# Letting 128-row products run as four column tiles of 32, so that tiling runs join

## The chip, the cores and the metric

The kernel runs on one core of a Trainium2 chip. The metric is device time in microseconds (us), from the first to the last instruction of the program on that core. A core has a matrix engine (PE, TensorE), which multiplies a stationary operand that it has loaded (PEld) by a moving operand and writes to PSUM; a vector engine (DVE), a scalar engine (ACT), a general engine (POOL), and a queue (SP) that issues transfers by DMA.

PE can work as one array of 128 rows by 128 columns, or as several smaller arrays side by side: two row tiles of 64 rows, two column tiles of 64 columns, or four column tiles of 32 columns. Its tiling mode is a property of each product, and going from one mode to another costs something.

## The reference

Two layers of a recurrent, memory-augmented attention block (A) alternate with two gated feed-forward blocks (B), on 2048 tokens of 448 features; each block has a layer norm before it and a residual sum after it.

```python
# A: 64 segments of 32 tokens, one after another; 8 memory rows are carried along
for s in range(n_seg):
    h = concatenate([mem, xs])                   # 8 + 32 rows of 448
    q, k, v = h @ Wq, h @ Wk, h @ Wv             # 16 heads of 256
    p = softmax(where(mask, q @ k.T / 16, -1e9))
    o = (p @ v) @ Wo
    mem = o[:8]                                  # goes into the next segment
    outs.append(o[8:])
# B
gate, up = x @ W_gate, x @ W_up                  # 448 -> 1792
out = (gate * (gate > 0) * up) @ W_down          # 1792 -> 448
```

The loop over segments is serial through `mem`: a segment's memory rows need the whole attention of the segment before.

## The kernel before, in words

**Folded weights.** At the start the kernel multiplies Wq by Wk, and Wv by Wo, per head (`products` in `setup`), so that a step works with 448-wide matrices M and N alone. The weights are loaded in quarters, by transposing transfers (`wT`) and plain ones (`wo`), in the order in which the calls stand.

**Steps.** Both attention layers run in one loop of 68 steps, the second layer four segments behind the first. A step t does, in the code's names:

- `t_units`: h times M, as batches `tH` (two row tiles of 64, for the last 64 of the 448 features) and `tF` (full array, the other 384);
- `s_mem`, batch `smem`: scores of the memory rows, 5 products per layer of 40 columns (8 memory and 32 segment keys); softmax; `p_t_mem`, batch `ptm`: one transpose by a product with the identity;
- `u_mem` (`umem`, row tiles) and `un_mem` (`unm`): the value sums of the memory rows, 28 groups of four products, each on one column tile of 32 (mode COLS4);
- `m_t`, batch `mt`: five small transposing products that bring the new memory rows into the layout of the next step;
- `s_seg`, batch `sseg`: scores of the segment rows, 14 products per layer, most of 40 columns; softmax; `u_seg` (`useg`, row tiles);
- every second step `un` (`una`, `unb`): the value sums of two segments, groups of four column-tile products of 448 columns, and `glu` with batches `glH` (row tiles), `glF` (gate and up products, full array, 128 columns) and `dn` (down products, full array, 448 columns).

**Who sets the order.** Nothing is ordered by hand at run time: a planner (`_Order`) writes the order of every engine when the kernel is built. `turns` fixes the order of PE's batches by ranks (`RANK`) and by which batches are ready and have a PSUM bank. `run` then goes through time with estimated costs, adds `SWITCH` (100 ns) where a PE batch has another mode than the one before, and fills the other engines' orders. A batch is given to `mm` with a mode: FULL, ROWS, COLS2 or COLS4. One batch alone has an alternative: `mt` may run as ROWS where it comes after ROWS (the argument `alt`). Every matmul is issued in `_Sched.pe`, so all of them carry line 135 in the profile, and groups are told apart by their tiles: `hT,TTm` is smem, `hT,TTs` sseg, `ident,Pm` ptm, `selm,X` mt, `Nw,UTm` unm, `Nw,big` un, `xBT,big` glF (128 rows) or glH (64 rows), `big,hB` dn, `PTs,hK` useg, `PTm,hK` umem.

A batch waits for its semaphores at its first weight load and signals at its last matmul.

Of the kernel before, what the change touches and what calls it, by code (L numbers as in the profile page):

```python
# [13 lines left out]
D = 448  # L14
# [158 lines left out]
class _Order:  # L173
# [76 lines left out]
    def turns(self):  # L250
# [38 lines left out]
            fire(o)  # L289
        return order[::-1]  # L290

    def run(self):
        self.graph()
        free = {e: 0.0 for e in self.ENGS}
        mode = 0
        cand = {e: [] for e in self.ENGS}
        banks = {b: 0.0 for b in range(8)}
        bankt = {}

        def activate(o):  # L300
            o.ready = {e: self.ready_at(o, e) for e in o.eng}
            for e in o.eng:
                cand[e].append(o)

        for o in self.ops:
            if o.np == 0:
                activate(o)
        order = []
        turn = self.turns()
        total = len(self.ops)  # L310
        busy = {e: 0.0 for e in self.ENGS}
        last = self.LAST

        def at(o, e):
            t = o.ready[e]
            if t < free[e]:
                t = free[e]
            if o.alloc:
                n = len(o.alloc)
                if len(banks) < n:  # L320
                    return None
                x = sorted(banks.values())[n - 1] + last[e]
                if x > t:
                    t = x
            elif e != "pe":
                for tl, q in o.bq:
                    d = bankt.get((tl.bank, q))
                    if d:
                        for src, x in d.items():
                            if src != e and x + last[e] > t:  # L330
                                t = x + last[e]
            return t

        while len(order) < total:
            best = None
            for e in self.ENGS:
                lst = []
                for o in cand[e] if e != "pe" else turn[-1:]:
                    t = at(o, e) if o.np == 0 else None
                    if t is not None:  # L340
                        lst.append((t, o))
                if not lst:
                    continue
                lim = max(free[e], min(lst, key=lambda x: x[0])[0]) + SLACK[e]
                bt, bo = 0.0, None
                for t, o in lst:
                    if t <= lim and (bo is None or o.prio > bo.prio or (o.prio == bo.prio and o.i < bo.i)):
                        bt, bo = t, o
                if best is None or bt < best[0]:
                    best = (bt, e, bo)  # L350
            if best is None:
                raise RuntimeError("no operation can go: the buffers are held in a cycle")
            t, e, o = best
            if len(o.eng) > 1:
                for e2 in o.eng:
                    if e2 != e:
                        t2 = at(o, e2)
                        if t2 is not None and t2 + o.cost[e2][0] < t + o.cost[e][0]:
                            t, e = t2, e2
            for tl in o.alloc:  # L360
                b = min(banks, key=lambda k: (banks[k], k))
                del banks[b]
                tl.bank = b
                for q in ALLQ:
                    bankt[(b, q)] = {}
            dur, occ = o.cost[e]
            if e == "pe":
                turn.pop()
                if mode == o.alt:
                    o.mode = mode  # L370
                elif o.mode != mode:
                    dur += self.SWITCH
                    occ += self.SWITCH
                    mode = o.mode
            o.fixed = e
            o.start = t
            busy[e] += occ
            free[e] = t + occ
            o.fin = t + dur
            for tl, q in o.bq:  # L380
                d = bankt[(tl.bank, q)]
                if d.get(e, 0.0) < o.fin:
                    d[e] = o.fin
            for tl in o.tiles:
                tl.left -= 1
                if tl.left == 0:
                    banks[tl.bank] = max(max(bankt[(tl.bank, q)].values(), default=0.0) for q in ALLQ)
            for e2 in o.eng:
                cand[e2].remove(o)
            for q in o.succs:  # L390
                q.np -= 1
                if q.np == 0:
                    activate(q)
            order.append(o)
        self.span = max(o.fin for o in order)
        self.busy = busy
        self.order = order
# [155 lines left out]

def TR(out, src, ident):
    return (out, src, ident, dict(is_transpose=True))

# [3 lines left out]
class _Kernel:  # L562
# [222 lines left out]
    def setup(self):  # L785
# [72 lines left out]
        for q in range(4):  # L858
            products(q, (0, 1, 4, 5)[q], (2, 3, 6, 7)[q], True)
        wT(0, S.Wv_d, 0)  # L860
        wo(2, 0)
        wo(3, 1)
        wT(1, S.Wv_d, 1)
        wT(4, S.Wv_d, 2)
        wo(6, 2)
        wo(7, 3)
        wT(5, S.Wv_d, 3, half=0)
        wT(5, S.Wv_d, 3, half=1)
# [131 lines left out]
    def s_mem(self, t):  # L1000
# [3 lines left out]
        nl = l1 - l0  # L1004
        T = S.tile()

        def mms():
            out = []
            for l in range(l0, l1):
                v = T.b()[:, l * KEYS:l * KEYS + KEYS]  # L1010
                for c in range(3):
                    out.append(MM(v, S.TTm[:, l, c * 8:c * 8 + 8, :, :].rearrange("p i s q -> p (i s q)"), S.hT[:, b, c, l, 0:KEYS], start=(c == 0)))
                for odd in range(2):
                    w = S.TTm3[:, l, 1 - odd:17 - odd, :].rearrange("p i q -> p (i q)")
                    out.append(MM(v, w, S.hT[:, b, 3 + odd, l, 0:KEYS], stop=(odd == 1)))
            return out

        S.mm("smem", mms, nl * 5 * 25.0, [("TTm", k, st) for k in range(5) for st in range(2)] + S.hkeys(b), T.res())
        src = lambda: T.b()[:, l0 * KEYS:l1 * KEYS].rearrange("p (l x) -> p l x", l=nl)
        st, F = S.stat, S.Fm  # L1020
        dst = S.Pm[:, :].rearrange("p (l x) -> p l x", l=2)[:, l0:l1, 0:KEYS]
# [8 lines left out]
    def s_seg(self, t):  # L1030
# [3 lines left out]
        nl = l1 - l0  # L1034
        T = S.tile()

        def mms():
            v = T.b()[:, 0:8 * KEYS].rearrange("p (s g l x) -> p s g l x", s=2, g=2, l=2)
            out = []
            for l in range(l0, l1):  # L1040
                for g in range(2):
                    for c in range(3):
                        for st in range(2):
                            i = c * 8 + 4 * g
                            out.append(MM(v[:, st, g, l, :], S.TTs[:, l, st, i:i + 4, :].rearrange("p u q -> p (u q)"), S.hT[:, b, c, l, 0:KEYS], start=not out))
                    out.append(MM(v[:, :, g, l, :], S.TTs[:, l, g, 24:28, :].rearrange("p u q -> p (u q)"), S.hT[:, b, 3:5, l, 0:KEYS],
                                  stop=(l == l1 - 1 and g == 1)))
            return out

        S.mm("sseg", mms, nl * (12 * 25.0 + 2 * S.pitch(80)) + 12.0, [("TTs", k, st) for k in range(5) for st in range(2)] + S.hkeys(b), T.res())  # L1050
        full = nl == 2
        v = lambda ap: ap if full else ap[:, l0:8:2, :]
        src = lambda: v(T.b()[:, 0:8 * KEYS].rearrange("p (a x) -> p a x", a=8))
# [27 lines left out]
    def p_t_mem(self, t):  # L1081
        S = self
        T = S.tile()
        S.mm("ptm", lambda: [TR(T.b().bitcast(BF)[:, 0:128], S.Pm[:, :], S.ident[:, :])], 60.0, [("Pm",), ("ident",)], T.res())
        S.cp("ptmE", lambda: S.PTm[:, :], lambda: T.b().bitcast(BF)[:, 0:128], 128, T.res(), [("PTm",)], speed=1.9)

    def u_mem(self, t):
# [63 lines left out]
    def m_t(self, t):  # L1151
# [6 lines left out]
        T = S.tile()  # L1158
        def mms(mode):
            r = slice(0, 64 if mode == ROWS else 128)  # L1160
            return [MM(T.b()[:, 32 * i:32 * i + 32], S.X[r, c:c + 128], S.selm[r, :], start=True, stop=True) for i, c in enumerate((0, 128, 256, 384, 320))]

        S.mm("mt", mms, 5 * 25.0, [("X", 0), ("X", 1)] + [("sel", j) for j in range(3)], T.res(), alt=ROWS)
        for half, nb in ((0, 4), (1, 5)):
            r = slice(64 * half, 64 * half + 64)
            S.cp("mtE", lambda r=r, nb=nb: S.hT[r, b, 0:nb, l0:l1, SEG:KEYS],
# [83 lines left out]
    def glu(self, q, n):  # L1250
        S = self
        for k, (a, z) in enumerate(S.GU):
# [11 lines left out]

            S.mm(f"glH{k}", hm, w * S.pitch(n) + 8.0, [("xBT",), ("W3", 0), ("W3", 1)], G.res() + V.res() + [("hB", k)], mode=ROWS)
            for W, T, nm in ((S.Wg, G, "Wg"), (S.Wu, V, "Wu")):
                S.mm(f"glF{k}", lambda W=W, T=T, a=a, w=w, col=col: [MM(col(T, i), W[:, kt, (a + i) * 128:(a + i) * 128 + 128], S.xBT[:, kt, 0:n], stop=(kt == 2))
                                                                 for i in range(w) for kt in range(3)],
                     3 * w * S.pitch(n), [("xBT",)] + [(nm, kt) for kt in range(3)], T.res())
            S.act("glE", lambda E, G=G, k=k, w=w: E.activation(S.gT[:, k % 2, 0:w * n], G.b()[:, 0:w * n], ACT.Relu), w * n, G.res(), [("gT", k % 2)])  # L1270
            S.dve("glE", lambda E, V=V, k=k, w=w, a=a: E.tensor_tensor(S.hB[:, a:a + w, 0:n], S.gT[:, k % 2, 0:w * n].rearrange("p (i x) -> p i x", i=w),  # L1271
                                                                        V.b()[:, 0:w * n].rearrange("p (i x) -> p i x", i=w), ALU.mult),
# [2 lines left out]
        wd = [("Wd", 0), ("Wd", 1)]  # L1275
        if n == 128:
            for k in range(7):
                S.mm("dn", lambda k=k: [MM(T.b()[:, 0:D], S.hB[:, f, :], S.Wd[:, f, :], start=(f == 0), stop=(f == NFC - 1)) for f in (2 * k, 2 * k + 1)],
                     2 * S.pitch(D), [("hB", k // 2)] + wd, T.res())
        else:  # L1280
            for k in range(7):
                S.mm("dnc", lambda k=k: [MM(T.b()[32 * j:32 * j + 32, 0:D], S.hB[:, 2 * k + j // 2, 32 * (j % 2):32 * (j % 2) + 32], S.Wd[:, 2 * k + j // 2, :],
# [102 lines left out]
```

## Time and profile before

Three runs: median 1495.27 us (1492.01 to 1495.7). The profiled execution has a span of 1494.6 us.

| engine | busy us | share | instructions |
|---|---|---|---|
| PE, matmuls | 1451.1 | 97% | 37105 |
| PEld, weight loads | 1161.1 | 78% | 37105 |
| ACT | 802.3 | 54% | 2490 |
| DVE | 793.1 | 53% | 2036 |
| POOL | 38.6 | 3% | 86 |

| PE group | tiling | matmuls | busy us |
|---|---|---|---|
| tF, 80 columns | full | 10080 | 383.9 |
| un, 448 columns | 4 column tiles | 5488 | 282.8 |
| unm, 224 columns | 4 column tiles | 7504 | 193.3 |
| glF, 128 columns | full | 2436 | 156.7 |
| dn, 448 columns | full | 406 | 89.0 |
| sseg, 40 and 80 columns | full | 1792 | 104.6 (56.1 + 48.5) |
| smem, 40 columns | full | 635 | 26.9 |
| mt | full, or row tiles | 230 + 105 | 19.1 (13.3 + 5.8) |
| ptm | full | 67 | 15.1 |

Busy time of matmuls is the union of spans whose ends are modelled, and matmuls overlap; the distance from one start to the next says more on their cost than a mean length. A line of the timeline gives the start, the length, the engine, the tiles written and read, the tiling as rows*columns, the moving operand's shape, and how many instructions were merged; in brackets stand the idle time ahead and what ended it. "issue" there means that nothing in the profile explains the wait. The page's part on queues gives packets, MB and share for each DMA queue.

### The profile page before, as it was taken

Reading aid. Unit: us, or ns where it says so; the run is one execution under the profiler, and the core shown is the slowest. Engines: PE = TensorE matmul, PEld = TensorE weight load, DVE = VectorE, ACT = ScalarE, POOL = GpSimd, SP = SyncE. Lnnn points to the kernel's source line nnn. Section 1 sums busy time; section 2 is a strip of 40 time slices with the busy share of each in tenths; the row PEclk is TensorE's granted clock in tenths of the full one; section 3 lists DMA queues with packets and bytes.
Section 4 is the critical chain, followed back from the end, with each engine's and each line's share of the span. In section 5 each row is a group of like instructions: output and inputs, shape, how many; then the busy total and the mean of one; then the engine's idle time right before and its main releaser. Section 6 shows DMA issues by size and latency. Waiting matters only on the chain.

```text
span 1494.6 us, 79814 instructions
## 1 busy us (share of the span) xinstructions
PE 1451.1 (97%) x37105; PEld 1161.1 (78%) x37105; DVE 793.1 (53%) x2036; ACT 802.3 (54%) x2490; POOL 38.6 (3%) x86
## 2 busy tenths in 40 slices
PE   6889999999999999999999999999999999999998
PEld 2468777788878878788878878887878878887776
DVE  4435455546455555645555564646555564645454
ACT  6744555556455555555455545655455555645443
POOL 2000000000000000000000000000000000000000
PEclk9999999999999999999999999999999999999999
DMA  9842111121121111111212211111111211211121
GB/s 216 224 114 34 24 30 28 30 23 31 27 34 25 28 33 28 27 22 32 30 29 27 29 31 23 29 27 34 26 29 32 29 26 24 30 28 29 24 32 20
DMA packets 185708, 59.77 MB, mean 40 GB/s; under 512 B 174488, under 2 KB 184480, under 8 KB 185376
## 3 DMA queue, kind: packets, MB, share of 16 engines
q1 hardware_dynamic: 185264, 54.60, 20.4%
q8 instruction: 291, 4.77, 1.3%
q14 instruction: 41, 0.34, 0.1%
q10 hardware_dynamic: 112, 0.07, 0.0%
HBM read 10.33 MB, written 1.84 MB: 8 GB/s over the span
## 4 chain that ended last, share of the span: by engine, by line
PE 86%; DMA 6%; DVE 3%; SPq 2%; ACT 1%; issue 1%; POOL 0%
PE P L135 86%; DMA PTs<-Ps 2%; SPq L810 2%; DMA xBT<-xnB 2%; DMA RN<-RT 1%; DMA big<-in_A_Wk_dram 0%; DMA stg<-xnA 0%; ACT Mw L731 0%; ACT big L731 0%; DVE stat L915 0%; DVE X L1148 0%; DVE big L734 0%; ACT Fm L1024 0%; DVE XF L1234 0%; DVE XB L1236 0%
## 5 line engine op out<-in xcount | busy, mean ns | idle before, releaser
L135 PE MATMUL P<-hT,Mw 128*128 128x80 bf16 (+1 forms) x11424 | 421.1, 200 | 5.4 <-issue 5.4
L135 PEld LDWEIGHTS P<-hT,Mw 128*128 128x128 bf16 x11424 | 402.9, 100 | 14.4 <-issue 6.0
L135 PE MATMUL P<-Nw,big 128*32 128x448 bf16 x5488 | 282.8, 353 | 0.1
L731 ACT ACTIVATE TTs<-P 128x384 bf16<-128x384 f32 (+2 forms) x566 | 258.2, 456 | 0.0
L135 PE MATMUL P<-xBT,big 128*128 128x128 bf16 (+3 forms) x3920 | 213.0, 214 | 2.9 <-DMA xBT<-xnB 2.2
L135 PEld LDWEIGHTS P<-Nw,big 128*32 128x32 bf16 x5488 | 138.4, 97 | 96.9 <-issue 0.4
L731 ACT ACTIVATE TTm<-P 128x96 bf16<-128x96 f32 (+3 forms) x592 | 144.1, 243 | 121.4 <-PE P L135 111.9
L731 ACT ACTIVATE big<-P 128x512 bf16<-128x512 f32 (+1 forms) x343 | 169.4, 536 | 73.1 <-PE P L135 69.9
L135 PEld LDWEIGHTS P<-xBT,big 128*128 128x128 bf16 (+1 forms) x3920 | 183.5, 97 | 22.9 <-issue 7.7
L135 PE MATMUL P<-Nw,UTm 128*32 128x224 bf16 x7504 | 193.3, 260 | 2.5 <-DVE UTm L734 1.2
L135 PEld LDWEIGHTS P<-Nw,UTm 128*32 128x32 bf16 x7504 | 180.4, 97 | 16.3 <-issue 4.3
L734 DVE CAST TTm<-P 128x64 bf16<-128x64 f32 (+3 forms) x88 | 19.5, 221 | 244.2 <-PE P L135 244.1
L734 DVE CAST big<-P 128x512 bf16<-128x512 f32 (+1 forms) x169 | 106.6, 637 | 62.5 <-PE P L135 60.5
L1148 DVE TENSOR_TENSOR X<-P,XH 32x224 bf16<-32x224 f32 x134 | 51.0, 381 | 120.0 <-ACT XH L1145 117.7
L1145 ACT ACTIVATE XH<-P 64x224 f32<-64x224 f32 x67 | 23.6, 353 | 155.8 <-PE P L135 155.8
L135 PE MATMUL P<-big,hB 128*128 128x448 bf16 (+1 forms) x574 | 98.7, 353 | 0.2 <-DVE hB L1271 0.2
L1270 ACT ACTIVATE gT<-P 128x512 bf16<-128x512 f32 (+2 forms) x140 | 71.1, 510 | 46.9 <-PE P L135 26.0
L135 PE MATMUL P<-hT,M 64*128 64x80 bf16 (+1 forms) x3808 | 92.5, 196 | 3.3 <-ACT M L731 1.1
L135 PEld LDWEIGHTS P<-hT,M 64*128 64x128 bf16 x3808 | 74.8, 96 | 25.5 <-issue 7.3
L1271 DVE TENSOR_TENSOR hB<-gT,P 128x512 bf16<-128x512 bf16 (+2 forms) x140 | 80.0, 576 | 19.6 <-PE P L135 16.8
L135 PE MATMUL P<-PTs,hK 64*128 64x512 bf16 (+1 forms) x640 | 84.8, 337 | 5.1 <-DMA PTs<-Ps 5.1
L917 ACT ACTIVATE stat<-stat,cvec 128x1 f32<-128x1 f32 (+1 forms) x69 | 20.6, 298 | 91.3 <-DVE stat L916 90.0
(100 smaller groups left out, 1247.3 us busy)
## 6 DMA issues: line engine op xcount, KB each, us to landing
big<-in_A_Wo_dram SPq DMA_DIRECT2D x4, 896.0 KB, 6.5
out_dram<-ys SPq DMA_DIRECT2D x32, 56.0 KB, 2.0
XA<-in_A_x_dram SPq DMA_DIRECT2D x31, 56.0 KB, 2.2
big<-in_B_W_down_dram SPq DMA_DIRECT2D x2, 784.0 KB, 6.3
big<-in_B_W_gate_dram SPq DMA_DIRECT2D x3, 448.0 KB, 4.1
big<-in_B_W_up_dram SPq DMA_DIRECT2D x3, 448.0 KB, 3.6
hK<-hT SPq DMA_TRANSPOSE x67, 3.3
PTs<-Ps SPq DMA_TRANSPOSE x66, 2.8
```

Of the source, the lines that this page charges most:

```text
L135: ins = E.matmul(out, lhsT=lhsT, rhs=rhs, **kw)
L731: return E.activation(out(), src(), ACT.Copy, scale=scale or 1.0)
L734: return E.tensor_copy(out(), src())
L810: wload(f"w{k}" + ("ab"[half] if half is not None else ""), lambda E: E.dma_start_transpose(dst, W[:, c:c + w]), [("slot", i, j) for i in ...
L917: S.act(kind, lambda E: E.activation(st[rows, so + 9:so + 10], st[rows, so + 7:so + 8], ACT.Ln, bias=S.cvec[rows, 0:1], scale=1.0), 1, [(k ...
L1145: S.act("xE", lambda E: E.activation(S.XH[64:128, :], T.b()[64:128, 0:224], ACT.Copy), 224, T.res(BOTQ), [("XH",)])
L1148: S.dve("xE", lambda E, r=r, r2=r2, c=c: E.tensor_tensor(S.X[r, c], T.b()[r, 0:224], S.XH[r2, :], ALU.add), 224, T.res((j,)) + [("XH",)], ...
L1270: S.act("glE", lambda E, G=G, k=k, w=w: E.activation(S.gT[:, k % 2, 0:w * n], G.b()[:, 0:w * n], ACT.Relu), w * n, G.res(), [("gT", k % 2)])
L1271: S.dve("glE", lambda E, V=V, k=k, w=w, a=a: E.tensor_tensor(S.hB[:, a:a + w, 0:n], S.gT[:, k % 2, 0:w * n].rearrange("p (i x) -> p i x", ...
```

## The change

Products with 128 output rows may now be split into four products of 32 output rows, one on each column tile. A product in COLS4 mode and another in COLS4 mode need no change of mode between them, so smem, sseg, ptm, mt, glF and dn next to the value sums (`unm`, `un`) can run in the value sums' mode. `QUAD` makes the four products; `alt` is now a tuple of modes that a batch may have; and `tilings` goes through PE's order once before planning: a batch that can keep the mode of the one before keeps it, and otherwise it takes the mode that also serves most of the batches after it. The order of PE's batches and their ranks stay. Two weight loads of the setup also change places with others.

```diff
+    def tilings(order):
+        mode = 0
+        for i, o in enumerate(order):
+            may = o.alt or (o.mode,)
+            if mode not in may:
+                j = i + 1
+                while j < len(order) and len(may) > 1:
+                    both = [m for m in may if m in (order[j].alt or (order[j].mode,))]
+                    if not both:
+                        break
+                    may, j = both, j + 1
+                mode = may[0]
+            o.mode = mode
...
         turn = self.turns()
+        self.tilings(turn[::-1])
...
-                if mode == o.alt:
-                    o.mode = mode
-                elif o.mode != mode:
+                if o.mode != mode:
...
+def QUAD(mode, out, lhsT, rhs, **kw):
+    if mode != COLS4:
+        return [MM(out, lhsT, rhs, **kw)]
+    return [MM(out[32 * j:32 * j + 32], lhsT[:, 32 * j:32 * j + 32], rhs, **kw) for j in range(4)]
...
         wT(0, S.Wv_d, 0)
+        wT(1, S.Wv_d, 1)
         wo(2, 0)
         wo(3, 1)
-        wT(1, S.Wv_d, 1)
+        wo(6, 2)
         wT(4, S.Wv_d, 2)
-        wo(6, 2)
         wo(7, 3)
...
-                    out.append(MM(v, S.TTm[:, l, c * 8:c * 8 + 8, :, :].rearrange("p i s q -> p (i s q)"), S.hT[:, b, c, l, 0:KEYS], start=(c == 0)))
+                    out += QUAD(mode, v, S.TTm[:, l, c * 8:c * 8 + 8, :, :].rearrange("p i s q -> p (i s q)"), S.hT[:, b, c, l, 0:KEYS], start=(c == 0))
...
-        S.mm("smem", mms, nl * 5 * 25.0, [("TTm", k, st) for k in range(5) for st in range(2)] + S.hkeys(b), T.res())
+        S.mm("smem", mms, nl * 5 * 25.0, [("TTm", k, st) for k in range(5) for st in range(2)] + S.hkeys(b), T.res(), alt=(FULL, COLS4))
...
-        S.mm("mt", mms, 5 * 25.0, [("X", 0), ("X", 1)] + [("sel", j) for j in range(3)], T.res(), alt=ROWS)
+        S.mm("mt", mms, 5 * 25.0, [("X", 0), ("X", 1)] + [("sel", j) for j in range(3)], T.res(), alt=(FULL, ROWS, COLS4))
```

sseg, ptm, glF and dn are rewritten in the same way as smem, each with `alt=(FULL, COLS4)`; the planner's costs of these batches stay as they were.

More of the change, by code (lines that the diff above doesn't have):

```diff
@@ L290, in turns @@
         return order[::-1]
+    @staticmethod
+    def tilings(order):
[11 more added lines that the diff above has]
+            o.mode = mode
     def run(self):
@@ L1005, in s_mem, with mms @@
         T = S.tile()
-        def mms():
+        def mms(mode):
             out = []
@@ L1011, in mms @@
                 for c in range(3):
-                    out.append(MM(v, S.TTm[:, l, c * 8:c * 8 + 8, :, :].rearrange("p i s q -> p (i s q)"), S.hT[:, b, c, l, 0:KEYS], start=(c == 0)))
+                    out += QUAD(mode, v, S.TTm[:, l, c * 8:c * 8 + 8, :, :].rearrange("p i s q -> p (i s q)"), S.hT[:, b, c, l, 0:KEYS], start=(c == 0))
                 for odd in range(2):
                     w = S.TTm3[:, l, 1 - odd:17 - odd, :].rearrange("p i q -> p (i q)")
-                    out.append(MM(v, w, S.hT[:, b, 3 + odd, l, 0:KEYS], stop=(odd == 1)))
+                    out += QUAD(mode, v, w, S.hT[:, b, 3 + odd, l, 0:KEYS], stop=(odd == 1))
             return out
-        S.mm("smem", mms, nl * 5 * 25.0, [("TTm", k, st) for k in range(5) for st in range(2)] + S.hkeys(b), T.res())
+        S.mm("smem", mms, nl * 5 * 25.0, [("TTm", k, st) for k in range(5) for st in range(2)] + S.hkeys(b), T.res(), alt=(FULL, COLS4))
         src = lambda: T.b()[:, l0 * KEYS:l1 * KEYS].rearrange("p (l x) -> p l x", l=nl)
@@ L1035, in s_seg, with mms @@
         T = S.tile()
-        def mms():
-            v = T.b()[:, 0:8 * KEYS].rearrange("p (s g l x) -> p s g l x", s=2, g=2, l=2)
+        def mms(mode):
             out = []
@@ L1044, in mms @@
                             i = c * 8 + 4 * g
-                            out.append(MM(v[:, st, g, l, :], S.TTs[:, l, st, i:i + 4, :].rearrange("p u q -> p (u q)"), S.hT[:, b, c, l, 0:KEYS], start=not out))
-                    out.append(MM(v[:, :, g, l, :], S.TTs[:, l, g, 24:28, :].rearrange("p u q -> p (u q)"), S.hT[:, b, 3:5, l, 0:KEYS],
-                                  stop=(l == l1 - 1 and g == 1)))
-            return out
-        S.mm("sseg", mms, nl * (12 * 25.0 + 2 * S.pitch(80)) + 12.0, [("TTs", k, st) for k in range(5) for st in range(2)] + S.hkeys(b), T.res())
+                            v = T.b()[:, 0:8 * KEYS].rearrange("p (s g l x) -> p s g l x", s=2, g=2, l=2)[:, st, g, l, :]
+                            out += QUAD(mode, v, S.TTs[:, l, st, i:i + 4, :].rearrange("p u q -> p (u q)"), S.hT[:, b, c, l, 0:KEYS], start=not out)
+                    v = T.b()[:, 0:8 * KEYS].rearrange("p (s g l x) -> p s g l x", s=2, g=2, l=2)[:, :, g, l, :]
+                    out += QUAD(mode, v, S.TTs[:, l, g, 24:28, :].rearrange("p u q -> p (u q)"), S.hT[:, b, 3:5, l, 0:KEYS], stop=(l == l1 - 1 and g == 1))
+            return out
+        S.mm("sseg", mms, nl * (12 * 25.0 + 2 * S.pitch(80)) + 12.0, [("TTs", k, st) for k in range(5) for st in range(2)] + S.hkeys(b), T.res(),
+             alt=(FULL, COLS4))
         full = nl == 2
@@ L1083, in p_t_mem @@
         T = S.tile()
-        S.mm("ptm", lambda: [TR(T.b().bitcast(BF)[:, 0:128], S.Pm[:, :], S.ident[:, :])], 60.0, [("Pm",), ("ident",)], T.res())
+        S.mm("ptm", lambda mode: [(*m[:3], dict(is_transpose=True)) for m in QUAD(mode, T.b().bitcast(BF)[:, 0:128], S.Pm[:, :], S.ident[:, :])],
+             60.0, [("Pm",), ("ident",)], T.res(), alt=(FULL, COLS4))
         S.cp("ptmE", lambda: S.PTm[:, :], lambda: T.b().bitcast(BF)[:, 0:128], 128, T.res(), [("PTm",)], speed=1.9)
@@ L1160, in mms @@
             r = slice(0, 64 if mode == ROWS else 128)
-            return [MM(T.b()[:, 32 * i:32 * i + 32], S.X[r, c:c + 128], S.selm[r, :], start=True, stop=True) for i, c in enumerate((0, 128, 256, 384, 320))]
-        S.mm("mt", mms, 5 * 25.0, [("X", 0), ("X", 1)] + [("sel", j) for j in range(3)], T.res(), alt=ROWS)
+            return [m for i, c in enumerate((0, 128, 256, 384, 320))
+                    for m in QUAD(mode, T.b()[:, 32 * i:32 * i + 32], S.X[r, c:c + 128], S.selm[r, :], start=True, stop=True)]
+        S.mm("mt", mms, 5 * 25.0, [("X", 0), ("X", 1)] + [("sel", j) for j in range(3)], T.res(), alt=(FULL, ROWS, COLS4))
         for half, nb in ((0, 4), (1, 5)):
@@ L1266, in glu @@
             for W, T, nm in ((S.Wg, G, "Wg"), (S.Wu, V, "Wu")):
-                S.mm(f"glF{k}", lambda W=W, T=T, a=a, w=w, col=col: [MM(col(T, i), W[:, kt, (a + i) * 128:(a + i) * 128 + 128], S.xBT[:, kt, 0:n], stop=(kt == 2))
-                                                                 for i in range(w) for kt in range(3)],
-                     3 * w * S.pitch(n), [("xBT",)] + [(nm, kt) for kt in range(3)], T.res())
+                S.mm(f"glF{k}", lambda mode, W=W, T=T, a=a, w=w, col=col: [m for i in range(w) for kt in range(3) for m in QUAD(
+                    mode, col(T, i), W[:, kt, (a + i) * 128:(a + i) * 128 + 128], S.xBT[:, kt, 0:n], stop=(kt == 2))],
+                     3 * w * S.pitch(n), [("xBT",)] + [(nm, kt) for kt in range(3)], T.res(), alt=(FULL, COLS4))
             S.act("glE", lambda E, G=G, k=k, w=w: E.activation(S.gT[:, k % 2, 0:w * n], G.b()[:, 0:w * n], ACT.Relu), w * n, G.res(), [("gT", k % 2)])
@@ L1277, in glu @@
             for k in range(7):
-                S.mm("dn", lambda k=k: [MM(T.b()[:, 0:D], S.hB[:, f, :], S.Wd[:, f, :], start=(f == 0), stop=(f == NFC - 1)) for f in (2 * k, 2 * k + 1)],
-                     2 * S.pitch(D), [("hB", k // 2)] + wd, T.res())
+                S.mm("dn", lambda mode, k=k: [m for f in (2 * k, 2 * k + 1)
+                                              for m in QUAD(mode, T.b()[:, 0:D], S.hB[:, f, :], S.Wd[:, f, :], start=(f == 0), stop=(f == NFC - 1))],
+                     2 * S.pitch(D), [("hB", k // 2)] + wd, T.res(), alt=(FULL, COLS4))
         else:
```

## The prediction, made before the result was known

> **What bounds the kernel now.** I read the page's busy lines and the chain first, then the instructions by shape, then the timeline of PE (TensorE) in two stretches from the steady middle, and last the places where PE stood still for no semaphore.
>
> ```profile
> PE 1451.1 (97%) x37105; PEld 1161.1 (78%) x37105; DVE 793.1 (53%) x2036; ACT 802.3 (54%) x2490; POOL 38.6 (3%) x86
> PE 86%; DMA 6%; DVE 3%; SPq 2%; ACT 1%; issue 1%; POOL 0%
> q8 instruction: 291, 4.77, 1.3%
> ```
>
> PE is the bound: 97% busy, 86% of the chain that ended last. VectorE and ScalarE are half idle. So whatever shortens or lengthens the stream of PE instructions shows one to one. Keep the third line in mind: it is the queue that brings instructions, 291 packets of 16 KB. PE and PEld hold 74210 instructions; 4.77 MB / 74210 = 64 bytes each, and 74210 / 291 = 255 in a packet. So this queue is PE's instruction supply, in packets of 256.
>
> ```profile
> 706.28 0.41 PE L135 MATMUL P<-hT,TTm 128*128 128x40 bf16 x10
> 706.53 0.91 PE L135 MATMUL P<-hT,TTs 128*128 128x40 bf16 x28
> 707.28 1.50 PE L135 MATMUL P<-xBT,big 128*128 128x128 bf16 x24
> ...
> 738.67 2.86 PE L135 MATMUL P<-Nw,UTm 128*32 128x224 bf16 x112
> 741.46 1.51 PE L135 MATMUL P<-xBT,big 128*128 128x128 bf16 x24
> 742.82 0.29 PE L135 MATMUL P<-selm,X 128*128 128x32 bf16 x5
> 742.96 0.83 PE L135 MATMUL P<-xBT,big 128*128 128x128 bf16 x12
> 743.72 0.39 PE L135 MATMUL P<-PTs,hK 64*128 64x512 bf16 x2
> ```
>
> Columns: start, length, then the tiling as rows*columns (128*128 full, 64*128 row tiles, 128*32 four column tiles). The 10 score products of smem take 706.53 - 706.28 = 0.25 us, 25 ns each; the 28 of sseg 0.75 us; a gate product 1.34 / 24 = 56 ns; a group of four column-tile products of unm (738.67 to 741.37 or so) 2.7 / 28 = 96 ns. From 738.67 on the change's kind of place: column tiles, then gate products and the transposes mt as full products, then row tiles.
>
> **Starvation.** PE has idle time that the profile lays to nothing:
>
> ```profile
> 1430.72 0.34 PE L135 MATMUL P<-hT,Mw 128*128 128x40 bf16 x7
> 1431.82 0.55 PE L135 MATMUL P<-hT,Mw 128*128 128x40 bf16 x16 [0.76 <-issue]
> ...
> 85.56 0.54 PE L135 MATMUL P<-hT,Mw 128*128 128x40 bf16 x15 [0.63 <-issue]
> ...
> 49.24 0.55 PE L135 MATMUL P<-hT,Mw 128*128 128x40 bf16 x11 [3.66 <-issue]
> ```
>
> These cut through one batch of products, where no wait stands. Counting PE and PEld records from the start, the stalls that end at 49.23, 85.56, 101.70, 154.48 and 1431.82 us stand before records 705, 1729, 2497, 5569 and 71617; each of these plus 63 is a multiple of 256 (3, 7, 10, 22, 280 packets). And each ended 1.30 to 1.50 us after an instruction packet had landed. PE ran out of instructions there. Over all 291 packets: a packet takes 0.9 to 1.6 us (mean 1.08) and starts about 1.2 us after the stream issued, 64 records ahead of what runs, enters the packet before it (10 to 25% mark of that lag, 1.15 to 1.28; the least is 0.96). With 1.4 us from landing to use, a packet is usable **3.7 us** after its request, and until then PE lives on 256 + 64 = 320 instructions. So starvation begins where 320 instructions run in less than 3.7 us, below **11.6 ns each**. The densest 320 of the kernel before take 3.55 us: it stands just at the edge.
>
> **What the skill says.** "TensorEngine Tiling (Array Packing)", Key Properties: a change of tiling mode drains TensorE; the trace agrees and prices it: over all 722 changes of mode the first matmul comes a median of 90 to 98 ns later than its pitch. The same page, Restrictions: column tiling turns off Fast Weight Load; no trace line shows what a short column-tile product then costs, so I bound it below. "TensorE: Matmul & The Clock Gate", Back-to-back issue gap: products never start closer than about 25 ns, and its table of facts gives a queue 64 deep; the trace agrees with the 25 ns and with a lead of about 64. "Runtime: NRT & Kernel Launch", Instruction fetch mechanics: instructions come in 16 KiB blocks of 256, fetched while the block before runs, and the cost is "mostly hidden". The block size agrees; the same section gives PE room for 2048 instructions, but the trace refills one block ahead and starves, and the measurement decides.
>
> **The change, part by part.**
> (1) Mode changes removed. I took the order of PE's batches from the trace (ranks decide it, and they stay) and applied the new rule batch by batch. 722 changes become 630: 92 x 95 ns = **-8.7 us**. Turned to column tiles are 31 of 68 sseg batches (840 products), 17 of 67 smem (165), 74 of 280 gate/up batches (684), 43 of 68 mt (215), 18 ptm and 1 down batch: 1924 products in all.
> (2) Instructions added. Each turned product is 4 loads + 4 matmuls in place of 1 + 1: +5772 matmuls and loads, 11544 instructions, 45 packets more.
> (3) Pace of a group of four. Lower bound: no slower than one full product (25 ns at 40 columns, 56 at 128). Row tiles do that: the pairs of tH with 40 columns start 25 ns apart, so the floor is per tile and not per instruction; and at a run's start four load+matmul pairs of unm are issued 3.4 ns apart, 14 ns for the four. Upper bound: unm issues four loads per 96 ns, so if loads went one after another, up to 24 ns each, a group would cost 96. I take the lower bound, **0 us**, since four tiles are shown to issue and stream together; the upper bound is 1005 x 71 ns (smem, sseg) + 684 x 40 ns (gate) = +98 us.
> (4) Instruction supply. Eight instructions in 25 ns are 3.1 ns each, in 56 ns 7.0: both below 11.6. A turned sseg batch is 224 instructions in 0.75 us; the other 96 of the 320 at the steady mean (85 us for 4357 records, 19.5 ns) give 1.9; 2.6 against 3.7 starves PE 1.1 us. A turned gate stretch of three batches is 288 instructions in 2.0 us, plus 0.6: again 1.1 us. 31 + 74/3 such stretches x 1.1 = 61 us, less where a stretch is split between two packets, more where smem stands ahead of sseg or unm (12 ns) and tH (9 ns) are the neighbours. Replaying all recorded start times with the turned products at eight instructions, and each packet usable 3.0 to 4.0 us after its request, gives 35 to 65 us in 45 to 60 stalls; I take **+50**. The same replay of the kernel before gives nothing up to 3.7.
> (5) Given back: while PE starves, the other engines catch up on its semaphore waits (some 30 us over the span, half of that in the first 250 us): **-4 us**.
> (6) Setup order. wT(1) now goes ahead of two Wo loads on SyncE's queue, so the first value products get Wo some 4 to 8 us later; in the trace Wo is issued at 37.0 and lands 6.5 us later, and the first value product runs at 51.0. What slack there is hides it: **0, +-2 us**. The planner's estimates of time shift too, so ScalarE and VectorE share copies differently; both are half idle: 0.
> Sum: 1495.3 - 8.7 + 50 - 4 = **1532.6**, say 1532.
>
> **Rivals.** *A, the supply keeps up* (0.12): only the changes of mode count, 1486. For it: 1 packet in 60 starves now, mostly in the first 160 us where loads fill the DMA engines. Against: the stall at 1431.8 has only the step's own transposes beside it, and 224 instructions in 0.75 us are four times denser than anything now run. *B, column-tile loads go one after another* (0.12): +98 - 9 = 1584; at 12 ns per instruction starvation is as rare as in unm. For it: without Fast Weight Load the loads are unproved at this pace. Against: (3). *C, supply starves but only where smem and sseg fill a packet* (0.04): about 9 us, which cancels the gain, 1495. *Forecast* (0.72): starvation of 35 to 65 us.
>
> **How the numbers follow.** The forecast's own span is 1518 to 1548, wider to both sides because the lag of a packet behind other DMA traffic is uneven (up to 2.9 us). To hold 8 in 10 the range leaves out A and the far part of B: 1498 to 1565. Slower 0.84 (forecast, B), faster 0.13 (A and a little), same 0.03.
>
> **What would show it.** After: PE near 42900 instructions; q8 near 336 packets; the wait of PE for "issue" up from 5.4 us to some tens, the stalls again at multiples of 256, most beside 128*32 products with 40 or 128 columns; 630 mode changes. In the timeline a turned sseg batch starts its groups 25 ns apart (step 3 right) or near 100 (B). If "issue" stays near 5 us, step 4 is wrong. PE's busy share should fall, though PE stays the bound.

## The result, and the profile after

The changed kernel takes 1567.22 us (median of 4 runs, 1564.83 to 1570.42) against 1495.49 us for the kernel before beside it: a ratio of **1.0484** with a 95% interval of 1.0456 to 1.0511, or +71.7 us. The forecast had the direction and the mechanism, and 1532 us; the time lies above its range.

The page of the changed kernel, the lines that answer to those shown of before (busy time and instructions by engine, the chain, the instruction queue):

```profile
PE 1468.1 (94%) x42877; PEld 1181.9 (75%) x42877; DVE 792.9 (51%) x2049; ACT 799.4 (51%) x2477; POOL 38.5 (2%) x86
PE 86%; issue 4%; DVE 3%; DMA 3%; SPq 2%; ACT 1%; POOL 0%; DVEq 0%
q8 instruction: 336, 5.51, 1.5%
```

PE has 5772 more matmuls and as many more weight loads, and the instruction queue 45 more packets. PE's busy time rose by only 17 us while the span grew by 71.6; its share fell from 97% to 94%, and "issue" stands in the chain with 4%, four times as much as before. The view of waits, PE's own, says the same (engine, what it waited for, us in total, times, longest):

```profile
PE P L135 <- issue: 60.9, 72, 2.2
```

It was 5.4 us in 4 waits. The view counts only time in which no matmul is modelled to run; from start to start, as in the table below, the same gaps are longer. By shape, with the idle time ahead of each group behind the last bar:

```profile
L135 PE MATMUL P<-hT,Mw 128*128 128x80 bf16 x10080 | 385.7, 202 | 17.3 <-issue 17.2
L135 PE MATMUL P<-hT,TTs 128*32 128x40 bf16 x2880 | 36.3, 186 | 10.4 <-issue 10.3
L135 PE MATMUL P<-xBT,big 128*32 128x128 bf16 x2040 | 35.8, 219 | 9.8 <-issue 9.8
L135 PE MATMUL P<-hT,TTs 128*32 128x80 bf16 x480 | 27.4, 203 | 6.0 <-issue 5.9
L135 PE MATMUL P<-xBT,big 128*32 128x64 bf16 x696 | 7.6, 199 | 1.9 <-issue 1.9
```

Some 28 of the 60.9 us stand ahead of turned products (128*32 with 40 to 128 columns), and the largest single group, 17.2 us, ahead of tF, which the change did not touch: what starves is whatever comes when the packet ends, often just after the dense stretch. The timeline of PE shows two such places:

```profile
701.19 0.55 PE L135 MATMUL P<-Nw,big 128*32 128x448 bf16 x8
701.57 0.29 PE L135 MATMUL P<-selm,X 128*32 128x32 bf16 x20
701.70 0.60 PE L135 MATMUL P<-hT,TTs 128*32 128x40 bf16 x45
702.64 0.71 PE L135 MATMUL P<-hT,TTs 128*32 128x40 bf16 x67 [0.34 <-issue]
703.29 0.39 PE L135 MATMUL P<-PTs,hK 64*128 64x512 bf16 x2
703.51 0.59 PE L135 MATMUL P<-hT,M 64*128 64x80 bf16 x24
704.04 1.39 PE L135 MATMUL P<-hT,Mw 128*128 128x80 bf16 x34
706.77 0.41 PE L135 MATMUL P<-hT,Mw 128*128 128x80 bf16 x7 [1.33 <-issue]
```

The value sums `un`, the transposes `mt` and the scores `sseg` now run in one mode: the joining works. But the 112 matmuls of one sseg batch are cut at the 45th, where no semaphore stands, and the next packet ends within a tF batch, 4.13 us later (706.77 - 702.64). In between PE runs 67 + 2 + 24 + 34 = 127 matmuls, 128 loads and one semaphore instruction: 256.

**Where the time went.** I sorted every distance from one matmul's start to the next, in both traces, into the pitch of its shape, changes of mode, waits for semaphores, and gaps of over 100 ns at the records whose count plus 63 is a multiple of 256. The count takes in PE's own semaphore instructions (431 before, 444 after); so do the record numbers of the prediction, which names PE and PEld alone.

| us | before | after | difference |
|---|---|---|---|
| gaps at packet ends (7, then 93 of them) | 6.6 | 82.2 | +75.6 |
| changes of mode (722, then 630) and everything by which the pace leaves the pitch | 86.1 | 83.3 | -2.8 |
| waits for semaphores | 42.5 | 41.1 | -1.4 |
| pitch of all shapes | 1349.5 | 1349.5 | 0 |
| span | 1494.6 | 1566.2 | +71.6 |

Some 10 us of each span lie before the first matmul's start and after the last one's. 92 changes of mode at 95 ns are -8.7 us, so the rest of that row, some +5.9 us, is laid to the turned products' own pace. Between matmuls of one shape, with no semaphore to wait for, 72 distances in the changed kernel are over 200 ns longer than the pitch: all 72 stand at a packet's end, none elsewhere. So the loss sits at packet ends and not in each added instruction. A stretch without such a gap shows the pace of turned products:

```profile
1131.92 0.30 PE L135 MATMUL P<-selm,X 128*32 128x32 bf16 x20
1132.05 0.85 PE L135 MATMUL P<-xBT,big 128*32 128x128 bf16 x48
1132.83 0.39 PE L135 MATMUL P<-PTs,hK 64*128 64x512 bf16 x2
```

Five groups of mt take 0.13 us, 26 ns each. Twelve gate groups take 0.78 us; less 95 ns for the change of mode at their end that is 57 ns each.

### The profile page after: what moved, and what is told of

Read it like the earlier page. It is cut to its first block, busy times and chain, and to the rows that moved or that the text cites. A ratio compares the mean times of both kernels' runs of the same rounds, so it can differ in the third digit from the quotient of the medians.

```text
span 1566.2 us, 91371 instructions
## 1 busy us (share of the span) xinstructions
PE 1468.1 (94%) x42877; PEld 1181.9 (75%) x42877; DVE 792.9 (51%) x2049; ACT 799.4 (51%) x2477; POOL 38.5 (2%) x86
## 4 chain that ended last, share of the span: by engine, by line
PE 86%; issue 4%; DVE 3%; DMA 3%; SPq 2%; ACT 1%; POOL 0%; DVEq 0%
PE P L135 86%; SPq L832 2%; DMA xBT<-xnB 1%; DMA PTs<-Ps 1%; DMA big<-in_A_Wo_dram 0%; DMA big<-in_A_Wk_dram 0%; ACT Mw L753 0%; ACT Fm L1046 0%; DMA RN<-RT 0%; DVE big L756 0%; DVE stat L937 0%; DVE XF L1259 0%; DVE X L1172 0%; DVE XB L1261 0%; DVE xnB L944 0%
## 5 line engine op out<-in xcount | busy, mean ns | idle before, releaser
L135 PE MATMUL P<-Nw,big 128*32 128x448 bf16 x5488 | 287.9, 354 | 2.9 <-issue 2.2
L135 PE MATMUL P<-xBT,big 128*32 128x128 bf16 (+5 forms) x5972 | 217.2, 214 | 13.9 <-issue 11.6
L135 PEld LDWEIGHTS P<-Nw,big 128*32 128x32 bf16 x5488 | 145.7, 97 | 97.3 <-issue 8.6
L135 PEld LDWEIGHTS P<-xBT,big 128*32 128x32 bf16 (+2 forms) x5972 | 187.0, 97 | 33.8 <-issue 19.3
L1295 ACT ACTIVATE gT<-P 128x512 bf16<-128x512 f32 (+2 forms) x140 | 71.1, 510 | 48.4 <-PE P L135 31.5
L135 PE MATMUL P<-hT,TTs 128*32 128x40 bf16 (+3 forms) x4312 | 69.6, 187 | 16.4 <-issue 16.2
```

Source lines behind the costliest of these rows:

```text
L135: ins = E.matmul(out, lhsT=lhsT, rhs=rhs, **kw)
```

## The experiments

Theory: PE's instructions come in packets of 256, one ahead; a stretch in which 256 are used up faster than the next packet comes starves PE. Rivals: each added instruction has a cost of its own, wherever it stands; column-tile products of few columns are slow; the order of the setup loads. After the result I corrected one thing in the replay (the recorded start times run again under a limited supply; the correction is told below) and set the delay of a packet to 3.85 us, so that the replay gives +73.3 us for the change itself. The expectations quoted are from that replay, fixed before each run.

**The same number of instructions, spread or in blocks.** Nothing is turned here; some batches of un have their 448-column products cut into four of 112. The two kernels differ only in which batches these are.

```diff
+            n_un = self.un_count = getattr(self, "un_count", -1) + 1
+            cut = 4 if n_un % 6 == 0 else 1          # spread
+            cut = 4 if n_un // 14 % 6 == 0 else 1    # block
+            wid = D // cut
...
+   S.N[:, o + j // 2, wid * z:wid * z + wid], ...) for o in (k, k + 2) for z in range(cut) for j in range(4)
```

> The kernel before, no batch turned; every sixth batch of un has its 448-column products cut into four of 112 columns (4 x 49 = 197 ns in place of 189), 5520 more instructions spread evenly, one dense batch of 0.4 us among five sparse ones. Starved supply: the four-fold batches are too short to use up a packet, net +2.4 us (1.8 from the cut itself), ratio 1.0015. Cost per added instruction (7 ns): +39 us. Column-tile products of few columns slow in themselves: the same as in the kernel with the cut batches in blocks.

> As the kernel with every sixth batch of un cut, but the cut batches stand together: all 14 batches of every sixth value sum, 6048 more instructions in stretches of 5.5 us at 6 ns per instruction. Starved supply: 3.5 packets in 5.5 us where one needs 3.85 us, net +62 us (54 to 66) in about 38 stalls, ratio 1.04. Cost per added instruction (7 ns): +42 us, and like the spread kernel. Slow column-tile products: as the spread kernel.

Measured: spread **1.0058** (1.0039 to 1.0077), 1501.4 against 1492.8 us, +8.6; block **1.0408** (1.0378 to 1.0438), 1554.7 us, **+61.9**. Nearly as many added instructions, seven times the cost; for spread, 2.4 us had been expected. PE's waits, first of spread, then of block:

```profile
PE P L135 <- issue: 6.5, 10, 3.9
```

```profile
PE P L135 <- issue: 49.8, 35, 3.3
```

The timeline of the block kernel shows the supply by itself:

```profile
106.97 0.48 PE L135 MATMUL P<-Nw,big 128*32 128x112 bf16 x23
108.56 1.11 PE L135 MATMUL P<-Nw,big 128*32 128x112 bf16 x73 [1.11 <-issue]
...
110.47 0.62 PE L135 MATMUL P<-Nw,big 128*32 128x112 bf16 x34
112.04 1.75 PE L135 MATMUL P<-Nw,big 128*32 128x112 bf16 x126 [0.94 <-issue]
113.58 0.26 PE L135 MATMUL P<-Nw,UTm 128*32 128x224 bf16 x2
115.49 2.86 PE L135 MATMUL P<-Nw,UTm 128*32 128x224 bf16 x110 [1.65 <-issue]
118.10 0.45 PE L135 MATMUL P<-Nw,big 128*32 128x112 bf16 x18
118.94 0.26 PE L135 MATMUL P<-Nw,big 128*32 128x112 bf16 x5 [0.40 <-issue]
```

PE restarts at 108.56, 112.04, 115.49 and 118.94 us: 3.48, 3.45 and 3.45 us apart. From 112.04 to 115.49 there are 126 + 2 matmuls with as many loads: 256 instructions. This decides against the cost per instruction and against slow column-tile products, for both rivals expected the two kernels to be alike: the same products, in nearly the same number, cost 8.6 us spread and 61.9 together. The spread kernel starves more than foreseen: 11.8 us at packet ends against 6.6 before. The replay has none of those 6.6 us either, and why it misses such small losses stays open.

**About as many instructions as the change, at 12 ns each.** Every product of un cut into two, the rest as in the two kernels above.

```diff
+            cut = 2
```

> The kernel before with every product of un cut into two of 224 columns: 10976 more instructions, about as many as the change adds (11544), at 12 ns each during all value sums, no batch turned. Starved supply (3.85 us per packet, 15 ns per instruction): a packet of 256 takes 3.07 us of value sums and starves by up to 0.8 us, net +22 us (9 to 32 for 3.65 to 3.95 us), ratio 1.015. Cost per added instruction (7 ns): +77 us. A threshold at 11.6 ns as the prediction had it: no more than the 3 us of the cut, ratio 1.002.

Measured: **1.0185** (1.0158 to 1.0213), 1523.7 against 1495.5 us, +28.2. This is the threshold test: 12 ns per instruction, above the 11.6 that the prediction named, starves PE all the same. The gaps at packet ends in its profile also come to 28.2 us, 21.6 more than before. With the fitted delay the limit is nearer 15 (3.85 us / 256). PE's wait:

```profile
PE P L135 <- issue: 16.7, 31, 3.8
```

**Parts of the change.** The changed kernel with some batches held to the full array:

```diff
-   smem, sseg:   alt=(FULL, COLS4)
+   smem, sseg:   alt=(FULL,)          # first kernel
-   glF, dn:      alt=(FULL, COLS4)
+   glF, dn:      alt=(FULL,)          # second kernel
+   smem, sseg, glF, dn: alt=(FULL,)   # third kernel
```

> The changed kernel with the score batches (smem, sseg) kept as full-array products; mt, ptm, gate/up and down batches may still turn. Starved supply (each packet of 256 instructions usable 3.85 us after the stream enters the packet before it, no lead carried over a stall), replayed on the recorded starts of before: 665 mode changes, 5364 more instructions, about 30 stalls, net +28 us over before (21 to 32). Cost per added instruction, wherever it stands (80 us / 11544 = 7.0 ns, less the mode changes saved): +32. Slow column-tile products: in proportion to turned products, some +36.

> The changed kernel with the gate/up and down batches kept as full-array products; mt, ptm, smem and sseg may still turn. Starved supply: 653 mode changes, 6954 more instructions, some 44 stalls, net +44 us over before (32 to 50), that is more than without the score batches although both add a similar number of instructions, because 25 ns for eight instructions is denser than 56 ns. Cost per added instruction: +42. Slow column-tile products: about +44.

> The changed kernel with only mt and ptm free to turn. Starved supply: 687 mode changes (35 fewer than before) and 1002 more instructions, too few in one place to starve: net -3.3 us, ratio 0.998. Cost per added instruction: +7.0 - 3.3 = +3.7 us, ratio 1.0025. Setup order as the cause of a part of the loss: this kernel has the new order of loads, so it would keep that part.

Measured: without the score batches **1.0249** (1.0223 to 1.0275), 1532.4 against 1497.0 us, +35; without the gate, up and down batches **1.0282** (1.0263 to 1.0302), 1537.8 us, +41; with mt and ptm alone **0.9969** (0.9958 to 0.9980), 1490.7 us against 1497.0. The ratio makes that some -5 us. So each dense family does its own damage, and the two that add few instructions do none. The instruction queue brings 312, 318 and 295 packets (291 before). PE's waits, one fence for each kernel in the same order:

```profile
PE P L135 <- issue: 28.7, 30, 2.4
```

```profile
PE P L135 <- issue: 42.8, 43, 2.0
```

```profile
PE P L135 <- issue: 1.7, 2, 0.9
```

The first kernel lost more than foreseen (35 against 28, with 21 to 32 as the range). Its gaps at packet ends are 38.1 us, +31.5 over before, near what was foreseen (28 and 57 changes of mode saved, some 33). PE's waits, "issue" aside, are 37.2 us in its profile against 33.3 before, which the theory doesn't have. The planner shares copies between ScalarE and VectorE in another way here; but it does so in the kernel with mt and ptm alone too, where these waits are 32.5 us, so the cause stays open. These first two runs alone would not have decided against a cost per instruction, which foresaw +32 and +42.

**The order of the setup loads.**

```diff
         wT(0, S.Wv_d, 0)
+        wT(1, S.Wv_d, 1)
         wo(2, 0)
         wo(3, 1)
-        wT(1, S.Wv_d, 1)
+        wo(6, 2)
         wT(4, S.Wv_d, 2)
-        wo(6, 2)
```

> The kernel before with only the new order of the two pairs of setup loads. Starved supply: nothing to do with it, 0 within 2 us. Setup theory: some us slower, because the first Wo quarter waits behind another transposing load.

Measured: **0.9979** (0.9964 to 0.9994), 1493.6 against 1497.0 us. The order costs nothing; if anything it gains some 3 us, a little more than the 2 allowed for. So it has no part in the loss.

**Is there a gain to keep?** mt and ptm free to turn with the loads in the old order, and mt, ptm and smem with the new one:

> The kernel with only mt and ptm free to turn, but the setup loads in the old order. Starved supply: 35 fewer mode changes at 95 ns, no starvation added: -3.3 us, ratio 0.998. If the gain of the kernel with mt and ptm alone came from the order of the loads (-3.4 us by itself), this one is no faster than before: 1.000.

> mt, ptm and smem free to turn, new order of the loads. Starved supply: 4 more mode changes saved than with mt and ptm alone and 90 more instructions; alike within the error, ratio 0.997. It is the most that can be turned by kind without starving, by the replay.

Measured: 0.9994 (0.9979 to 1.0008) and 0.9994 (0.9979 to 1.0009), both 1494 against 1495.5 us. Against the two expected gains of 0.2 and 0.3% this is a miss, though 0.998 is still inside the first interval. The kernel with mt and ptm alone and the new order is the best measured and beats both kernels, by 0.31% over the one before. That the old order shows no gain would fit a gain that came from the loads; but then mt, ptm and smem with the new order should have kept it, and didn't. So whether the 0.31% belongs to the joining stays open. A gain of the whole 8.7 us wasn't found.

## Why the prediction was wrong in size

Step by step, in the prediction's numbering:

1. **Mode changes removed: right.** 630 are left, and the trace after prices one as before: a median of 90 to 98 ns, whichever two of column tiles, row tiles and full array it lies between.
2. **Instructions added: right**, 5772 matmuls and 45 packets, exactly.
3. **Pace of a group of four: nearly right.** At 128 columns the groups start 56 ns apart (median), as the full product does. At 40 columns smem keeps 25 ns, while the groups of sseg have a median of 33; over some 720 groups that is most of the +5.9 us of pace, far from the 98 us of rival B. The Trainium skill, "TensorE: Matmul & The Clock Gate", Back-to-back issue gap, gives about 25 ns as the least distance of products. The median group of smem in this trace keeps just that distance from the next one; within a group the products start closer, which fits a floor of each column tile.
4. **Instruction supply: the step that failed, by size.** The prediction took +50 us; the gaps at packet ends grew by **75.6 us**. Both the sum by hand and the replay had one fault: they granted PE "256 + 64 = 320 instructions" to live on, every time. The 64 that the stream is ahead of execution are there only while PE is fed. Once PE has run dry the lead is gone: in the changed trace, where one starved packet follows another, the next packet's transfer started 1.06 to 2.5 us after PE's restart, with a median of 1.17: the prediction's lag from request to transfer, here counted from the restart. In the replay I let each request start 64 records ahead of execution, even where that was earlier than the packet in between had arrived. A packet after a starved one then lasts 3.55 to 4.50 us, with a median of about 3.9: 3.9 us / 256 makes 15 ns per instruction, not 11.6.

   What the correction is worth by itself shows when the changed kernel's own starts, gaps taken out, are replayed. With 3.7 us per packet, starvation is 35 us with the lead kept and 58 with it lost; with 3.85 us, 42 and 75; the trace has 82.2. For the halves, at 3.85 us, it is 1 and 20, where the trace has 28.2. So the lead is the larger part of the miss, and the delay's 0.15 us the smaller.

   In the replay of before's starts, 3.85 us with the lead lost gives +82 us of starvation and, less the 8.7 us, +73.3 us net, where +71.7 was measured. The 3.85 is fitted to this result, and its closeness is in part luck: 82 is 6 us above the measured growth, and the 5.9 us of pace that the replay leaves out make up for it. Its test is that it then gave +62 for the block kernel (measured +61.9) and +22 for the halves (+28.2).
5. **Given back: smaller.** Waits for semaphores shrank by 1.4 us, not 4. Why so little was not tested.
6. **Setup order: right**, nothing lost.

Of the rivals, A (supply keeps up) is refuted by the gaps at packet ends and B (loads one after another) by the pace of the groups; B's aside that starvation is rare at 12 ns per instruction fails in the halves. C (only smem and sseg starve) is refuted by the kernel without score batches, whose gaps at packet ends come to 38.1 us. The range failed because its upper end was drawn by B and by the unevenness of a packet's delay, not by the doubt in the sum itself.

## What to carry to other kernels

On an engine that is busy all the time, count instructions per microsecond and not only time: here a stretch of 256 PE instructions (loads and matmuls) in under some 3.5 to 4 us waited for its instructions, whatever they were. Cutting a product into four cost the array little here (56 ns for 56 at 128 columns, 25 or 33 for 25 at 40) and takes four times the instructions; it did no harm only where the turned batches were few and short, and no gain beyond some 0.3% was seen. Gaps that cut through a batch, with "issue" as the cause and a multiple of 256 instructions between them, are the sign to look for; the kernel before had a few.

## What the runs showed of the hardware that was not expected

- PE's instruction supply has a rate of its own: in the block kernel 256 instructions per 3.45 us at best (13.5 ns each), in the changed kernel about 3.9 us at the median, and a starved PE restarted mostly 1.2 to 1.6 us after the packet's transfer ended. The Trainium skill, "Runtime: NRT & Kernel Launch", Instruction fetch mechanics, has the cost of a block's end as "mostly hidden"; in the changed kernel it was 82.2 us, 5% of the time, and in the kernel before 6.6 us.
- Four column tiles with 128 columns each run at the pace of one full product, a median of 56 ns, weight loads of 32 columns included.
- The group that starves is often not the one that is dense: 17.2 of the 60.9 us of "issue" stood ahead of tF's full products at 80 columns, which the change left alone.
